# A scan and two feed-forward layers on one core: layer 0's second matrix laid side by side, and a new order of issue

## The chip, the core and the metric

The kernel runs on one core of a Trainium2 chip. The core has five engines that run side by side and wait for each other by semaphores: TensorE (PE) for matrix products, which it accumulates in PSUM; VectorE (DVE), ScalarE (ACT) and GpSimd (POOL) for element-wise work; and SyncE (SP), whose queue issues most of the DMAs between memory and SBUF. A matrix product is a pair of a weight load (PEld) and a matmul. The metric is the device time of one execution in microseconds, the median of three runs.

## What is computed

Inputs are four sequences of 768 tokens with 8 heads of width 32. First a scan with a decaying state, in chunks; then two feed-forward layers of width 256 with a hidden width of 1024, each with a residual; the first has a layer norm ahead, the second a mixing of tokens by a product of two thin matrices.

```python
for c in range(nc):                              # chunks of the scan, per batch and head
    cum = np.cumsum(la, axis=-1)
    L = np.exp(cum[:, :, :, None] - cum[:, :, None, :]) * causal
    y_intra = ((Cc @ Bc.T) * L) @ xc
    y_inter = (Cc @ state) * np.exp(cum)[:, :, :, None]
    state = decay_full * state + sum_j(Bc_j * xc_j * decay_from_j)
    y[:, :, sl] = y_intra + y_inter
# layer 0                                        # layer 1
xn = (x - mu) / np.sqrt(var + 1e-06) * g_ln      u = x + (x.T @ U @ V).T
x = x + np.maximum(xn @ w_ch1, 0.0) @ w_ch2      out = u + np.maximum(u @ w_ch1, 0.0) @ w_ch2
```

## The kernel before, in words

**Attention.** The tokens are cut into 24 chunks of 128 (6 for each sequence). For each chunk PE makes C times B (`cb`), DVE scans the decays (`lt`, L833) and multiplies (`mm`), PE makes the chunk's output (`yps`) and the new state (`sps`, then `gst` on DVE), and ACT and DVE split the output into a high and a low part (`yhl`), since every product of a layer is made of float32r numbers in two parts. PE also transposes the output (`tps`) for the residual and the norm.

**Layers.** A layer works on blocks of 256 or 512 tokens, in the order that `ORDER` gives for both layers together. For each of the 8 blocks f of 128 hidden units it makes `hps` (`mm1`, L1099: six products, in which the high and low parts of weights and tokens are combined), ACT makes the high part of its positive values (`hh`, L1106), DVE the low part (`hl`, L1110), and `mm2` adds the second product to `acc`. In layer 0 `mm2` runs for each 128 tokens. For the keys in `WIDE` one product of 512 columns (L1124) takes the high and the low part of the second matrix at once, and one of 256 columns (L1126) adds `hl` times the high part; the two halves of `acc` are added at the end on DVE (`y1`, `y2`, L1177). The other keys take three products of 256 columns (L1131). Layer 1 uses L1137. There are 128 products of L1124: 16 tiles of 128 tokens in the wide keys, times 8 blocks.

**The second matrix of layer 0** is one tile `w02` in SBUF, [128, 2, NF, DM]: part, block f, column. Its four pieces (`w2_piece`) are loaded as 64-bit words (`raw`), converted by ACT (L493, L497) and DVE (L502), and split: ACT writes the high part (`hi`, L393), DVE the low part (`lo`, L396). L1124 reads `weights["w2"][:, :, f, :]`: two runs of 256 elements, 8 KB apart.

**Between the layers** comes `mixing`: a thin product (`gps`), its copy (`gp`), a product that spreads it (`rps`), its high and low parts (`gsk`), then `ups` (transposes L1231 and products L1234), which ACT and DVE turn into the high and low parts of layer 1's input (`uhl`) and a copy (`u`).

**What sets the order.** The kernel does not write its instructions in the order of the program. Each piece of work is added to a `Plan` with its engine, a cost, what it waits for, the PSUM banks that it takes from a ring of eight (`m`) and a due time. `issue` then runs through time with these costs and places on each engine the ready piece that is due first. Due times come from `ffn` for products (from `T0` on) and backwards along the dependencies for the rest; then `SHIFT` moves whole kinds of pieces, `OFFSET` single ones, and `FIRST` puts some loads at the head in its own order. `NEAR` is how far ahead of the earliest start a piece may be and still be preferred, `STAY` a bonus for staying with the kind of product that PE is at. Two loads of `FIRST` (`cst0` and `ra` of the first chunks, by `ACTQ`) go by ACT's queue, the others by SP's.

Of the kernel before, what the change touches and what calls it, by code (L numbers as in the profile page):

```python
# [9 lines left out]
F32R = mybir.dt.float32r  # L10
# [11 lines left out]
NF = DFF // 128  # L22
# [8 lines left out]
FIRST = ['cst0', ('bc0', 0), 'rows', ('ra', 0, 0), ('stk', 0), ('xb', 0), (('w1', 0, 1), 'ld'), ('stk', 2),  # L31
         'cst', (('w1', 0, 0), 'ld'), (('w2', 0, 0), 'ld'), ('ra', 0, 2)]
# [10 lines left out]
OFFSET = {(('w1', 1, 1), 'ld'): 62.3, ('scan', 7, 0): 59.5, ('cb', 10, 0): 17.4, (('w1', 1, 2), 'ld'): 45.7,  # L43
# [6 lines left out]
          ('mm2', 0, (3, 0), 7): 48.4, ('tps', 18): -13.2, ('mean', 0): 3.2, ('state', 16): 3.2, ('cb', 15, 1): 8.1,  # L50
          ('mm2', 0, (1, 0), 2): 46.4, ('ylo', 17): 43.7, ('ras', 2, 3): 38.2, ('mm2', 1, (1, 1), 6): 18.4,
          ('mm2', 1, (1, 0), 6): 6.2, ('mm1', 1, (1, 0), 7): -7.5, ('ulo', (3, 0), 0): -5.0,
          ('mm2', 0, (0, 1), 0): -45.1, ('rep', 0): 22.0, ('cb', 13, 0): 13.0, ('mult', 3, 0): -35.8, ('tps', 8): 17.2,
          ('yhi', 8): -8.5, ('ulo', (1, 1), 1): 2.6, ('intra', 11): -18.9, ('acc', 1, (0, 1), 0): 20.3,
          ('state', 6): -7.8, ('ras', 2, 1): 1.3, ('bw', 1): -5.5, ('mm1', 0, (0, 1), 3): 19.1,
          ('hh', 0, (3, 0), 1): 0.3, ('gps', (3, 0)): -21.7, ('mm1', 1, (1, 1), 6): 7.7, ('bw', 10): 35.8,
          ('mult', 5, 0): -7.8, ('yhi', 14): 10.2, ('state', 8): -28.0, ('yc', 1): -27.8, ('mm1', 0, (1, 0), 7): -5.0,
          ('stk', 17): 23.2, ('ras', 2, 5): -5.1, ('mm1', 1, (0, 1), 5): 14.4, ('intra', 6): -34.5,
          ('mm2', 1, (1, 0), 3): 26.3, ('mm2', 0, (0, 1), 7): -33.3, 'dummy': 2.9, ('scan', 0, 0): 12.3,
          ('gsk', 0): 57.9, ('hl', 0, (0, 0), 3): -24.5, ('cb', 16, 0): 3.1, ('cb', 17, 0): -17.1,  # L60
          ('mm2', 1, (2, 1), 0): 11.1, ('ras', 2, 2): -6.6, ('state', 1): -28.0, ('state', 13): 15.9, ('gst', 1): -3.6,
          ('yhi', 7): -29.8, ('bc', 23): -34.6, (('w2', 0, 1), 's'): 10.4, ('mean', 8): -8.0,
          ('mm1', 0, (0, 0), 1): -28.9, ('state', 3): -86.4, ('tps', 23): -12.3, ('scan', 13, 1): -3.4,
          ('cd_', 2, 0): -11.7, ('yhi', 10): -33.1, (('w2', 1, 3), 'a'): -20.4, ('state', 19): -60.8,
          ('mm1', 0, (0, 0), 0): -34.7, (('w2', 1, 0), 's'): -45.9, (('w2', 1, 2), 's'): -35.8,
          ('mm1', 1, (3, 0), 3): -35.1, ('ylo', 5): -1.2, ('mult', 17, 1): -4.6, ('mult', 11, 0): -25.2,
# [11 lines left out]
          ('stk', 13): -2.8, ('sqrt', (0, 1)): 13.6, ('newton', (1, 1)): 38.2, ('y2', (0, 0), 1): 10.7,  # L78
# [7 lines left out]
          ('out', (3, 1), 1, 0): 13.5, ('acc', 1, (3, 0), 0): -27.5, ('out', (1, 0), 1, 0): -22.2,  # L86
          ('p2', (3, 1), 1, 0): 0.8, ('yhi', 5): -11.5, ('ylo', 18): -5.2, ('scan', 21, 0): 33.9,
# [4 lines left out]
          ('mm2', 0, (0, 0), 6): -1.6, ('sqrt', (3, 1)): -2.4, ('state', 22): -55.2, ('uhi', (0, 1), 1): 9.9,  # L92
          ('rst', 0, 0): -0.1, ('mult', 10, 0): -7.1, ('scan', 12, 0): 8.0, ('mm2', 1, (0, 1), 2): 0.2,
          ('tps', 20): -8.7, (('w1', 1, 3), 'f'): 18.9, (('v', 0), 'l'): 17.9, ('hh', 1, (1, 0), 6): 0.3,
          ('var', 23): -2.9, ('bcz', 0): -16.0, ('mm1', 1, (2, 1), 5): 29.3, ('mm1', 0, (3, 0), 5): 5.4,
          ('uhi', (2, 0), 1): 8.0, ('ras', 3, 0): 4.4, ('gst', 4): -2.3, ('slo', 2, 0): -4.0,
# [51 lines left out]
         "000 001 010 011 101 110 021 111 030 031 121 130 131".split()]  # L148


LAT, PER, T0, NEAR, SWITCH, STAY = 0.287, 1, -15.1, 0.11, 0.056, 2.68
dve = lambda n: 0.065 + n / 960
scn = lambda n: 0.06 + n / 480
dve2 = lambda n: 0.065 + n / 1920
# [1226 lines left out]
```

## Time and profile before

| | |
|---|---|
| median of 3 runs | 362.39 us (361.13, 362.39, 363.9) |
| the profiled execution's own time | 362.53 us |
| its span, first to last instruction | 360.3 us |
| PE busy | 352.9 us, 98% |
| DVE, ACT, POOL busy | 236.9, 160.8, 41.3 us |

A row of the trace is a group of instructions with its start, its busy time, engine, line and tile. Matmuls are pipelined and their ends are modelled, so the next one starts before the record of one ends: what a product costs in a stream is the step from start to start. "Idle before" is time in which the engine had nothing, with the engine and tile that ended it.

### The profile page before, as it was taken

To read this page: it belongs to the slowest core of one execution; us is meant where nothing else is said; L and a number is where in the kernel's file an instruction comes from. 1 tells how busy PE (TensorE), PEld (TensorE's weight loads), DVE (VectorE), ACT (ScalarE), POOL (GpSimd) and SP (SyncE) were. 2 spreads that over 40 slices of the span, in tenths; PEclk is the share of its full clock that TensorE was granted. 3 is DMA by queue.
4 is the path that set the end of the run, shared out by engine and by line. 5 is a ranking of instruction groups with operands and counts; after the bars stand their busy time and mean duration, and the time that the engine had idled before them with its cause. 6 is when DMAs were issued, how large, how long until landed. Compare 5 with 4: busy or idle time off the path is not lost.

```text
span 360.3 us, 7505 instructions
## 1 busy us (share of the span) xinstructions
PE 352.9 (98%) x2939; PEld 282.6 (78%) x2939; DVE 236.9 (66%) x503; ACT 160.8 (45%) x425; POOL 41.3 (11%) x44
## 2 busy tenths in 40 slices
PE   8999999999999999999999999999999999999995
PEld 4677787777799968877788888777787878888884
DVE  6888999989995545857998363867553562432423
ACT  3799665768853412425362121424423443231311
POOL 5545825202000000000030000000000000000000
PEclk9999999999999999999999999999999999999999
DMA  6999536474554436036452201715000000100101
GB/s 175 301 263 247 164 120 205 125 243 131 201 220 133 178 129 204 24 126 183 129 157 69 65 0 41 208 58 169 3 0 1 3 0 0 60 0 0 38 22 58
DMA packets 29592, 40.10 MB, mean 111 GB/s; under 512 B 3838, under 2 KB 19758, under 8 KB 29558
## 3 DMA queue, kind: packets, MB, share of 16 engines
q1 hardware_dynamic: 28982, 39.20, 34.9%
q8 instruction: 23, 0.38, 0.4%
q10 hardware_dynamic: 576, 0.43, 0.4%
q14 instruction: 11, 0.09, 0.1%
HBM read 31.67 MB, written 7.95 MB: 110 GB/s over the span
## 4 chain that ended last, share of the span: by engine, by line
PE 79%; DVE 9%; DMA 5%; ACT 3%; issue 2%; SPq 1%; DVEq 0%; ACTq 0%
PE hps L1099 32%; PE acc L1137 18%; PE acc L1124 7%; PE acc L1126 4%; PE acc L1131 3%; DMA raw<-in_w 3%; DMA lt<-arows 2%; PE yps L903 2%; PE cb L849 2%; DVE lt L833 2%; PE pc L523 2%; PE ups L1231 2%; DVE w L502 2%; PE tps L1025 1%; DVE hl L1110 1%
## 5 line engine op out<-in xcount | busy, mean ns | idle before, releaser
L1110 DVE SCALAR_TENSOR_TENSOR hl<-hps,hh 128x512 fp32r<-128x512 f32 (+1 forms) x104 | 66.4, 643 | 71.4 <-ACT hh L1106 71.2
L1106 ACT ACTIVATE hh<-hps 128x512 fp32r<-128x512 f32 (+1 forms) x104 | 58.3, 565 | 117.9 <-PE hps L1099 89.3
L1099 PE MATMUL hps<-yhl,w 128*128 128x512 f32 (+1 forms) x336 | 71.2, 364 | 0.6 <-DVE hl L1110 0.6
L1099 PE MATMUL hps<-uhl,w 128*128 128x512 f32 x288 | 69.3, 392 | 0.0
L1099 PEld LDWEIGHTS hps<-yhl,w 128*128 128x128 f32 x336 | 55.7, 189 | 11.8 <-DVE hl L1110 1.1
L1137 PE MATMUL acc<-hh,w 128*128 128x512 f32 x192 | 63.1, 392 | 0.0
L1099 PEld LDWEIGHTS hps<-uhl,w 128*128 128x128 f32 x288 | 53.4, 188 | 11.2 <-issue 0.2
L1124 PE MATMUL acc<-w,hh 128*128 128x512 f32 x128 | 47.6, 408 | 0.4 <-DVE hl L1110 0.3
L1137 PEld LDWEIGHTS acc<-hh,w 128*128 128x128 f32 x192 | 36.1, 188 | 7.4
L833 DVE TENSOR_TENSOR_SCAN lt<-lt,eye 128x512 f32<-128x512 f32 x32 | 39.3, 1239 | 3.5 <-DMA lt<-arows 3.4
L1137 PE MATMUL acc<-hl,w 128*128 128x512 f32 x96 | 37.4, 390 | 0.0
L1126 PE MATMUL acc<-w,hl 128*128 128x256 f32 x128 | 36.0, 281 | 0.2 <-DVE hl L1110 0.2
L807 POOL TENSOR_SCALAR stp<-stp,parity 128x256 f32<-128x256 f32 x23 | 28.2, 1240 | 22.5 <-DMA stp<-in_cbT 22.5
L1124 PEld LDWEIGHTS acc<-w,hh 128*128 128x128 f32 x128 | 24.0, 188 | 6.6 <-DVE hl L1110 0.5
L1126 PEld LDWEIGHTS acc<-w,hl 128*128 128x128 f32 x128 | 24.2, 189 | 0.9 <-DVE hl L1110 0.6
L1131 PE MATMUL acc<-w,hh 128*128 128x256 f32 x128 | 23.4, 283 | 0.0
L862 DVE TENSOR_TENSOR mm<-cb,lt 128x512 f32<-128x512 f32 x24 | 15.9, 687 | 7.7 <-PE cb L849 7.3
L1137 PEld LDWEIGHTS acc<-hl,w 128*128 128x128 f32 x96 | 18.1, 188 | 3.6
L1131 PEld LDWEIGHTS acc<-w,hh 128*128 128x128 f32 x128 | 20.3, 191 | 0.5
L602 POOL TENSOR_SCALAR ra<-ra 128x768 f32<-128x768 f32 x3 | 8.3, 2778 | 100.4 <-DMA ra<-in_a_rep 100.4
L1131 PE MATMUL acc<-w,hl 128*128 128x256 f32 x64 | 18.2, 285 | 0.0
L1177 DVE SCALAR_TENSOR_TENSOR yt<-acc,vrq,yt 128x256 f32<-128x256 f32 x40 | 17.2, 475 | 0.8 <-PE acc L1126 0.6
(110 smaller groups left out, 412.3 us busy)
## 6 DMA issues: line engine op xcount, KB each, us to landing
raw<-in_w SPq DMA_DIRECT2D x16, 512.0 KB, 5.2
lt<-arows SPq DMA_DIRECT2D x12, 512.0 KB, 4.9
stk<-st SPq DMA_DIRECT2D x48, 96.0 KB, 2.5
st<-sh SPq DMA_DIRECT2D x8, 384.0 KB, 3.0
xt<-in_xb SPq DMA_DIRECT2D x14, 192.0 KB, 3.7
lt<-arows SPq DMA_DIRECT2D x16, 128.0 KB, 4.8
xt<-in_xb SPq DMA_DIRECT2D x20, 96.0 KB, 3.7
stp<-in_cbT SPq DMA_DIRECT2D x12, 128.0 KB, 2.9
```

The lines of the kernel that those rows point to most:

```text
L602: eng.tensor_scalar(out=t, in0=t, scalar1=1e-6, scalar2=1.0, op0=ALU.max, op1=ALU.min)
L807: eng.tensor_scalar(out=t[:, 2 + i], in0=t[:, 1], scalar1=m, scalar2=None, op0=ALU.mult)
L833: V.tensor_tensor_scan(t, pair[k] if k < ROWS else t, eye, 0.0, op0=ALU.mult, op1=ALU.add)
L862: V.tensor_tensor(out=mm_[k][:, s_], in0=cbp[k, hf], in1=lt[k][:, s_], op=ALU.mult)
L1099: P.matmul(p[:, :n], w[:, k, fs], x[:, k, :], start=(i == 0), stop=(i == 5))
L1106: A.activation(out=hh[:, :n], in_=hps[l, key, f][:, :n], func=AF.Relu)
L1110: V.scalar_tensor_tensor(out=hl[:, :n], in0=hps[l, key, f][:, :n], scalar=0.0, in1=f32(hh[:, :n]), op0=ALU.max, op1=ALU.subtract)
L1124: P.matmul(accs[l, key][t], hh[:, at], weights["w2"][:, :, f, :], start=f == 0, stop=f == NF - 1, skip_group_check=True)
L1126: P.matmul(accs[l, key][t][:, DM:], hl[:, at], wh[:, f, :], start=False, stop=f == NF - 1, skip_group_check=True)
L1131: P.matmul(p, x[:, t * C:(t + 1) * C], w[:, f, :], start=(f == 0 and i == 0 and t % 2 == 0), stop=(f == NF - 1 and i == 2), skip_group_che ...
L1137: P.matmul(accs[l, key][d][:, :n], w[:, f, ds_], x[:, :n], start=(f == 0 and i == 0), stop=(f == NF - 1 and i == 2))
L1177: V.scalar_tensor_tensor(out=y, in0=p, scalar=rs[key]["r"][:, t:t + 1], in1=y, op0=ALU.mult, op1=ALU.add)
```

## The change

The tile of the second matrix becomes [128, NF, 2, DM]: for each block f the high and the low part lie side by side, and the wide product reads 512 elements in one run. The pieces are written with a step accordingly. The tables that set the order are replaced: `FIRST`, `OFFSET`, `T0`, `NEAR`, `STAY`, `SHIFT`. No operation is added or taken away. All lines of the changed kernel below `OFFSET` stand 4 later (L1128 for L1124).

```diff
-FIRST = ['cst0', ('bc0', 0), 'rows', ('ra', 0, 0), ('stk', 0), ('xb', 0), (('w1', 0, 1), 'ld'), ('stk', 2),
-         'cst', (('w1', 0, 0), 'ld'), (('w2', 0, 0), 'ld'), ('ra', 0, 2)]
+FIRST = [('bc0', 0), 'rows', ('stk', 0), ('xb', 0), (('w1', 0, 1), 'ld'), 'cst', 'cst0', ('stk', 2),
+         (('w1', 0, 0), 'ld'), (('w2', 0, 0), 'ld'), ('ra', 0, 0), ('ra', 0, 2)]
...
-OFFSET = {(('w1', 1, 1), 'ld'): 62.3, ('scan', 7, 0): 59.5, ('cb', 10, 0): 17.4, (('w1', 1, 2), 'ld'): 45.7,
+OFFSET = {(('w1', 1, 1), 'ld'): 69.1, ('scan', 7, 0): 41.9, ('cb', 10, 0): 1.6, ('mm1', 0, (1, 0), 3): 35.6,
...
-LAT, PER, T0, NEAR, SWITCH, STAY = 0.287, 1, -15.1, 0.11, 0.056, 2.68
+LAT, PER, T0, NEAR, SWITCH, STAY = 0.287, 1, 30.06, 0.108, 0.056, 1.03
...
-SHIFT = dict(zip("rows w0 w1 w2 ra0 ra chunk0 chunk".split(), [66.15, -409.01, -205.47, -39.12, -215.37, 82.47, -69.63, -11.6]))
+SHIFT = dict(zip("rows w0 w1 w2 ra0 ra chunk0 chunk".split(), [75.25, -477.95, -201.44, -29.96, -245.32, 76.45, -91.11, -12.35]))
...
-                weights["w2"] = const.tile([128, 2, NF, DM], F32R, tag="w02", name="w02")
-            return weights["w2"][:, i - 2]
+                weights["w2"] = const.tile([128, NF, 2, DM], F32R, tag="w02", name="w02")
+            return weights["w2"][:, :, i - 2]
...
-                        P.matmul(accs[l, key][t], hh[:, at], weights["w2"][:, :, f, :], start=f == 0, stop=f == NF - 1,
+                        P.matmul(accs[l, key][t], hh[:, at], weights["w2"][:, f].rearrange("p h d -> p (h d)"), start=f == 0, stop=f == NF - 1,
```

What the tables do to the order is seen on three places. Of the other engines' orders, SP's first rows differ in one pair (the load `cst` stands ahead of the second load of `stp` instead of behind it), and after that some loads of weight pieces, of `xt` and of `lt` change places by one or two.

**DVE, in the last blocks of layer 0's third group of tokens (`hl` with 256 columns).** `w<-w,raw` (L502) is the merge of a weight piece, `w<-w,w` the low part of one, `lt` the scan of a chunk. Before:

```order
L396 TENSOR_TENSOR yhl<-yps,yhl 128x2x64 x2
L396 TENSOR_TENSOR w_1071<-w_1482,w_991 128x512
L502 SCALAR_TENSOR_TENSOR w_1683<-w_1683,raw_1587 128x512
L1110 SCALAR_TENSOR_TENSOR hl<-hps,hh 128x256 x2
L833 SCALAR_TENSOR_TENSOR lt<-lt,eye 128x512
```

Now:

```order
L1114 SCALAR_TENSOR_TENSOR hl<-hps,hh 128x256
L506 SCALAR_TENSOR_TENSOR w_1589<-w_1589,raw_1349 128x512
L1114 SCALAR_TENSOR_TENSOR hl<-hps,hh 128x256
L400 TENSOR_TENSOR yhl<-yps,yhl 128x2x64 x2
L400 TENSOR_TENSOR w_1071<-w_1398,w_1021 128x2x256
L400 TENSOR_TENSOR w_1173<-w_1589,w_1153 128x512
L1114 SCALAR_TENSOR_TENSOR hl<-hps,hh 128x256
```

Before, two `hl` stood behind a merge; now one `hl` stands ahead of a merge, one behind it and one behind two more operations.

**PE, in the same blocks.** `acc<-w_369,hh` is the wide product, `hps` the first product of a block. Before:

```order
L924 MATMUL yps<-mm,xt_93 32x64 x16
L1124 MATMUL acc<-w_369,hh 128x512
L1126 MATMUL acc<-w_369,hl 128x256
L1124 MATMUL acc<-w_369,hh 128x512
L1126 MATMUL acc<-w_369,hl 128x256
L1099 MATMUL hps<-yhl,w_384 128x256
L1099 MATMUL hps<-yhl,w_301 128x256 x2
```

Now:

```order
L928 MATMUL yps<-mm,xt_93 32x64 x16
L1103 MATMUL hps<-yhl,w_384 128x256
L1103 MATMUL hps<-yhl,w_301 128x256 x2
L1103 MATMUL hps<-yhl,w_384 128x256
L1103 MATMUL hps<-yhl,w_301 128x256 x2
L1128 MATMUL acc<-w_369,hh 128x512
L1130 MATMUL acc<-w_369,hl 128x256
```

The pairs of the wide product moved behind a block of `hps`.

**PE, where the first mixing product `ups` for layer 1 stands.** Before, it stands among the `acc` products of the next block of tokens:

```order
L1131 MATMUL acc<-w_369,hh 128x256 x2
L1131 MATMUL acc<-w_369,hl 128x256
L1231 MATMUL ups<-cst,yt 128x128 x8
L1234 MATMUL ups<-vs,gsk 128x512 x2
L1131 MATMUL acc<-w_369,hh 128x256 x2
```

Now, among its `hps` products, after the second of five blocks:

```order
L1103 MATMUL hps<-yhl,w_384 128x512
L1103 MATMUL hps<-yhl,w_301 128x512 x2
L1235 MATMUL ups<-cst,yt 128x128 x8
L1238 MATMUL ups<-vs,gsk 128x512 x2
L1103 MATMUL hps<-yhl,w_384 128x512
```

It moved ahead of three blocks of `hps` and two of `acc`.

## Rows read from the trace of the kernel before

**Rows 1.** The page: busy time of the engines; the granted clock by slices.
```profile
PE 352.9 (98%) x2939; PEld 282.6 (78%) x2939; DVE 236.9 (66%) x503; ACT 160.8 (45%) x425; POOL 41.3 (11%) x44
PEclk9999999999999999999999999999999999999999
```

**Rows 2.** Stretches: length, then busy us and instructions of each engine, clock, DMA.
```profile
0.00:36.00 36.00, 34.14 (x496) 23.89 (x497) 29.16 (x74) 27.29 (x72) 19.36 (x29) 1.00 0.89 246
36.00:90.00 54.00, 52.47 (x843) 41.84 (x843) 52.19 (x127) 37.00 (x105) 19.17 (x15) 1.00 0.53 165
90.00:108.00 18.00, 17.75 (x166) 15.34 (x165) 17.02 (x32) 12.52 (x33) 0.00 (x0) 1.00 0.56 212
108.00:342.00 234.00, 234.00 (x1378) 189.86 (x1377) 133.63 (x265) 81.40 (x213) 2.77 (x1) 1.00 0.24 76
342.00:360.30 18.30, 14.56 (x65) 11.72 (x63) 4.89 (x9) 2.63 (x5) 0.00 (x0) 1.00 0.13 43
```

**Rows 3.** PE's waits: for whom, us in total, times, longest.
```profile
PE hps L1099 <- DVE hl L1110: 0.6, 1, 0.6
...
PE acc L1124 <- DVE w L396: 0.2, 1, 0.2
```

**Rows 4.** Groups by line and shape: count, busy us, mean ns, idle before.
```profile
L1137 PE MATMUL acc<-hh,w 128*128 128x512 f32 x192 | 63.1, 392 | 0.0
L1124 PE MATMUL acc<-w,hh 128*128 128x512 f32 x128 | 47.6, 408 | 0.4 <-DVE hl L1110 0.3 <-DVE w L396 0.2
L396 DVE TENSOR_TENSOR w<-w,w 128x512 fp32r<-128x512 f32 x12 | 8.1, 678 | 0.1
L393 ACT ACTIVATE w<-w 128x512 fp32r<-128x512 f32 x12 | 7.6, 633 | 4.9 <-DVE w L502 4.9
```

**Rows 5.** Timeline of PE: start, busy us; first of sixteen pairs, and what follows.
```profile
187.72 0.39 PE L1124 MATMUL acc<-w,hh 128*128 128x512 f32 x1
...
193.36 0.86 PE L1099 MATMUL hps<-yhl,w 128*128 128x512 f32 x3
```

**Rows 6.** The chain that ended last: start, us, what.
```profile
37.07 1.02 PE cb L844 x16
...
96.74 6.83 PE hps L1099 x30
103.57 2.88 PE acc L1131 x24
...
216.16 5.44 PE acc L1137 x24
```

**Rows 7.** Timeline of the start: the load of constants, POOL's parts, PE's reader.
```profile
5.53 0.43 SPq L378 DMA_DIRECT2D cst<-in_consts  x1
...
10.73 3.84 POOL L807 TENSOR_SCALAR stp<-stp,parity 128x256 f32<-128x256 f32 x4 [2.80 <-DMA stp<-in_cbT]
...
19.57 1.09 PE L844 MATMUL cb<-stp 64*64 64x256 f32 x16
```

**Rows 8.** Timeline of PE near 92 us.
```profile
91.92 0.39 PE L1124 MATMUL acc<-w,hh 128*128 128x512 f32 x1
92.56 0.39 PE L1126 MATMUL acc<-w,hl 128*128 128x256 f32 x1 [0.25 <-DVE hl L1110]
```

**Rows 9.** Timeline of DVE near 92 us.
```profile
91.48 0.69 DVE L502 SCALAR_TENSOR_TENSOR w<-w,raw 128x512 int32<-128x512 int32 x1 [0.85 <-ACT raw L497]
92.09 0.75 DVE L1110 SCALAR_TENSOR_TENSOR hl<-hps,hh 128x256 fp32r<-128x256 f32 x2
```

**Rows 10.** Timeline of all engines from 96 to 112 us.
```profile
96.31 1.65 DVE L1177 SCALAR_TENSOR_TENSOR yt<-acc,vrq,yt 128x256 f32<-128x256 f32 x4
...
99.06 0.68 DVE L1110 SCALAR_TENSOR_TENSOR hl<-hps,hh 128x512 fp32r<-128x512 f32 x1
...
107.07 0.71 PE L1234 MATMUL ups<-vs,gsk 128*128 128x512 f32 x2
...
110.52 1.13 ACT L393 ACTIVATE u<-ups 128x512 f32<-128x512 f32 x2 [1.85 <-DVE uhl L396]
```

More of the change, by code (lines that the diff above doesn't have):

```diff
@@ L42 @@
 FIRST_TWO = [('w1', 0, 0), ('w1', 0, 1)]
-OFFSET = {(('w1', 1, 1), 'ld'): 62.3, ('scan', 7, 0): 59.5, ('cb', 10, 0): 17.4, (('w1', 1, 2), 'ld'): 45.7,
[6 rows of a table removed]
[L50 to L66, printed above, removed]
[11 rows of a table removed]
-          ('stk', 13): -2.8, ('sqrt', (0, 1)): 13.6, ('newton', (1, 1)): 38.2, ('y2', (0, 0), 1): 10.7,
[7 rows of a table removed]
-          ('out', (3, 1), 1, 0): 13.5, ('acc', 1, (3, 0), 0): -27.5, ('out', (1, 0), 1, 0): -22.2,
-          ('p2', (3, 1), 1, 0): 0.8, ('yhi', 5): -11.5, ('ylo', 18): -5.2, ('scan', 21, 0): 33.9,
[4 rows of a table removed]
[L92 to L96, printed above, removed]
[15 rows of a table removed]
-          ('ylo', 6): 2.4, ('bc', 17): 19.0, ('gps', (2, 1)): -13.3, ('yhi', 23): 15.5, ('ulo', (1, 0), 1): -9.8,
[7 rows of a table removed]
-          ('ylo', 4): 1.9, 'starts': -20.3, ('tps', 15): 7.4, ('yc', 6): 16.8, 'clip': -14.9, ('uhi', (0, 0), 1): 13.5,
[6 rows of a table removed]
-          ('mm2', 0, (0, 0), 5): 1.6, ('yhi', 2): 10.6, ('scan', 9, 0): -5.3, ('yhi', 3): -1.6, ('mult', 2, 0): 2.4,
[9 rows of a table removed]
-          ('gp', (0, 0)): -3.0, ('mult', 18, 0): 1.7, ('ras', 0, 0): -2.2, ('tps', 13): 1.5, ('stw', 3, 0, 2): 0.2,
-          ('yhi', 15): 4.6, ('scan', 14, 0): -1.8, (('w1', 1, 1), 'l'): -0.3, ('mm1', 0, (3, 1), 7): 0.2,
-          ('hh', 1, (1, 0), 5): 0.1, ('uhi', (3, 0), 1): -4.5, ('cd_', 3, 0): 0.9, ('scan', 17, 1): -0.5,
[5 rows of a table removed]
@@ new lines @@
+OFFSET = {(('w1', 1, 1), 'ld'): 69.1, ('scan', 7, 0): 41.9, ('cb', 10, 0): 1.6, ('mm1', 0, (1, 0), 3): 35.6,
+          ('mm2', 0, (0, 1), 4): 90.1, ('cb', 4, 0): 10.4, (('w2', 1, 0), 'l'): -22.0, ('state', 15): 8.4,
+          ('mm1', 1, (0, 1), 4): 77.3, ('state', 11): 17.1, ('intra', 12): -4.4, ('gps', (1, 0)): 27.8,
[5 rows of a table added]
+          'zero': 3.0, ('cb', 13, 0): 15.0, ('tps', 8): 17.2, ('ulo', (1, 1), 1): 4.6, ('intra', 11): -4.7,
+          ('acc', 1, (0, 1), 0): 20.3, ('state', 6): -8.3, ('mm1', 0, (0, 1), 3): 18.9, ('mm1', 1, (1, 1), 6): 7.7,
+          ('mult', 5, 0): -12.3, ('state', 8): -36.4, ('tps', 14): -8.2, ('yc', 1): -31.5, ('mm1', 0, (1, 0), 7): -1.6,
[4 rows of a table added]
+          ('mm1', 0, (0, 0), 1): -35.9, ('state', 3): -78.8, ('scan', 13, 1): -3.4, ('yhi', 10): -38.2,
[5 rows of a table added]
+          ('hl', 1, (0, 1), 1): -27.7, ('scan', 11, 0): 2.7, ('ras', 2, 4): -23.8, ('scan', 22, 1): 7.2,
+          ('var', 10): 15.6, ('mm1', 1, (3, 0), 1): -7.8, ('yc', 13): 16.5, ('mm2', 0, (1, 0), 3): -3.1,
+          ('mm1', 1, (1, 1), 5): -35.6, ('hl', 0, (0, 1), 7): 2.7, ('cb', 23, 0): -17.0, ('mm1', 1, (0, 1), 2): 12.3,
+          ('hh', 0, (0, 1), 5): -5.1, ('yhi', 21): 18.5, ('stk', 13): 3.3, ('acc', 1, (3, 1), 1): 0.0,
[9 rows of a table added]
+          ('hl', 0, (1, 1), 3): 36.0, ('acc', 0, (1, 0), 1): 26.9, ('state', 20): -12.7, ('acc', 1, (1, 0), 0): -11.1,
[5 rows of a table added]
+          ('ylo', 13): 12.9, ('cb', 22, 1): 4.3, ('acc', 1, (2, 1), 0): 1.3, ('ylo', 6): 12.9, ('gps', (2, 1)): -14.1,
[3 rows of a table added]
+          ('acc', 1, (1, 0), 1): -19.5, ('tps', 21): -10.0, 'starts': -12.0, ('tps', 15): 7.4, ('yc', 6): 16.8,
[5 rows of a table added]
+          ('ylo', 22): -15.8, ('shi', 2, 1): 23.1, ('hh', 1, (3, 0), 3): 4.5, ('mean', 11): -5.9, ('ylo', 15): -3.6,
[13 rows of a table added]
+          ('intra', 15): 1.0, ('hh', 1, (1, 0), 6): 24.0, ('ylo', 20): 13.4, ('gm', 0): 0.3, ('mean', 17): -3.7,
[7 rows of a table added]
+          ('mm2', 1, (1, 1), 1): -4.9, ('ylo', 14): 0.9, ('stw', 3, 0, 2): 8.7, ('acc', 0, (0, 1), 1): 1.5,
[3 rows of a table added]
+          ('rep', 2): -10.6, ('out', (2, 1), 1, 0): 11.8, ('hh', 0, (2, 1), 0): 0.2, ('stm', 20): 18.3,
+          ('mm1', 1, (3, 0), 2): -4.4, ('gp', (3, 0)): -2.8, ('stk', 15): -3.8, ('mean', 15): -2.8,
+          ('gps', (3, 1)): 0.4, ('acc', 0, (3, 0), 1): 0.3, ('tps', 20): -1.0, ('part', 4, 3): -11.6,
+          ('ras', 3, 1): -10.1, ('mean', 23): -1.5, ('stw', 2, 0, 2): 12.3, (('w2', 0, 0), 'a'): 4.4,
+          ('bc', 22): -12.0, ('hh', 1, (1, 1), 6): -16.7, ('hh', 1, (0, 1), 2): -2.9, ('scan', 21, 0): 11.6,
+          ('ups', (0, 0), 0): -8.7, ('mean', 5): -7.7, ('hh', 0, (1, 1), 3): 0.9, ('stw', 3, 0, 1): 6.3,
+          ('yc', 7): -8.6, (('w2', 1, 3), 'h'): -6.1, ('sqrt', (2, 1)): -5.7, ('mult', 18, 1): 1.8, ('gst', 12): -1.6,
+          ('stk', 22): 7.3, ('var', 5): -3.9, ('intra', 19): -2.4, ('var', 9): -6.5, ('ulo', (2, 0), 0): -12.6,
+          ('y1', (3, 1), 3): 3.2, ('hl', 0, (1, 0), 5): -14.1, ('mm1', 0, (3, 0), 4): -8.1, (('w1', 0, 2), 'p'): -5.4,
+          ('acc', 1, (1, 1), 1): -16.3, ('stw', 3, 1, 2): -6.4, ('p2', (0, 0), 1, 0): -4.5, ('mult', 21, 1): -6.2,
[5 rows of a table added]
+          ('scan', 3, 0): -4.2, ('intra', 3): 1.0, ('intra', 5): 8.5, ('mm1', 0, (1, 1), 7): 2.3, ('cd', 0): 9.8,
[14 rows of a table added]
```

148 rows, old and new, of the table OFFSET are left out of this document.

## The prediction

> **What bounds the kernel now.** I read the page's busy shares first, then the table of stretches, then the list of what PE waited for, then single products. [...] The stretches say where the rest lies: from 108 to 342 us PE is busy 234.00 of 234.00, so nothing there can be late for it; the not-busy time is 1.86 us before 36, 1.53 us between 36 and 90, 0.25 us between 90 and 108, and 3.74 us in the last stretch, which is the drain after the last product [rows 2]. VectorE (DVE) is the second: 52.19 of 54 us between 36 and 90 and 17.02 of 18 between 90 and 108, but 134 of 234 after that [rows 2]. So the end is set by the sum of PE's products, plus what DVE makes PE wait for before 108. The waits view names eight waits of PE beside the start, from 0.6 down to 0.2 us [rows 3]. A matmul's record is longer than the step to the next one (0.39 against 0.227 us below), so each wait can hide up to 0.16 us more: 8 x 0.16 = 1.3 us. All that a better order can win on PE after 36 us is therefore about 1.53 + 0.25 + 1.3 = 3.1 us.
>
> **The count of instructions.** Both programs issue the same number of instructions of each line on each engine, the fillers at the start included, and groups of layer products and of attention products alternate 90 times on PE before and 92 times now. No term comes from removed or added work.
>
> **The layout.** 128 wide products (L1124) take 512 columns that lie in two runs of 256 elements, 8 KB apart; now they lie in one run. A record of theirs means 408 ns, a 512-column product whose columns lie together (L1137) 392 ns [rows 4]. Durations overlap, so I take the step instead. Sixteen pairs L1124 and L1126 stand back to back from 187.72 to 193.36 us [rows 5]: 5.64/16 = 352.5 ns a pair. Contiguous products cost 5.44/24 = 226.7 ns for 512 columns and 2.88/24 = 120.0 ns for 256 [rows 6], so a contiguous pair should cost 346.7 ns. The difference, 5.8 ns, times 128 is 0.74 us, all on the engine that sets the end. Bounds: zero, if the pair is slow for another reason than its strip, and 128 x 16 ns = 2.0 us by the records. I take 0.8, by the step, since the step is what adds up.
> [...]
> The other side of the edit: the pieces of layer 0's second matrix are now written as two runs instead of one. That is 4 conversions on ScalarE (ACT) and 4 subtractions on DVE. The rows of these lines already mix one-run and two-run writes, and mean 633 and 678 ns [rows 4]. I see no cost; were it 50 ns each, 4 x 0.05 = 0.2 us would fall on DVE while it is nearly full. Zero.
>
> **The start.** PE's own order is word for word the same up to the third group of cb products at 37.07 us [rows 6]; only then does a sps group change its place. On SP's queue one load of constants is moved ahead of a pair of stp loads. Its issue takes 0.43 us, so stp lands that much later; POOL, which waits 2.80 us for it, would start at 11.2 instead of 10.7 and end at 15.0, and PE reads the result at 19.57 us [rows 7]. Covered by 4.5 us; without that cover it would cost the 0.43. On DVE two pairs of small operations swap, with the same end. Zero for this stretch, so its 1.86 us stay.
>
> **The moved products before 96 us.** Here is the one wait that the new order goes at. From 91.92 to 92.56 PE takes 0.64 us for a product whose step is else about 0.23 (the pair less 0.12), waiting for an hl [rows 8]. That hl stands on DVE behind a merge of a weight piece (L502), and DVE stood idle 0.85 us until ACT had made its input [rows 9]. In the new order an hl stands ahead of such a merge and another behind it, the last of these loads stands one place earlier on SP, and PE places twelve more 256-column products ahead of four pairs. I count this wait as gone: 0.64 - 0.23 = 0.4 us. Bounds: 0 to 3.1 us won, as above; lost, if a merge is late in its new place too, the same 0.85 us of idle DVE in front of one hl. I stay near the small end, because only this one place shows both the cause and its removal. If it goes, the next late thing is the scan L833 behind it on DVE, which no product needs at once.
>
> **The move of ups.** PE issued the mixing products ups behind 30 hps and 24 acc products; now they stand between the second and third block of hps. They are the same products, 0 on PE itself. But ups takes two of the eight PSUM banks until ACT has copied u out: from 107.78 to 111.65 us, 3.9 us [rows 10]. Four y additions (96.31, 1.65 us), which free two banks of the previous sum, are spread on DVE behind two hl, a subtraction over 768 columns and each other. Two of the sum, two of ups and five of hps would be nine. Cover: five hps blocks take 6.83 us on PE [rows 6], so with ups (some 1.3 us) ahead of it the fifth is wanted at about 96.7 + 4 x 1.37 + 1.3 = 103.5 us, and before, DVE's first hl of the five began at 99.06 [rows 10]; even a few microseconds behind that a bank is free. I take 0; if the cover is gone PE waits at most the 3.9 us for which ups holds its banks. Queued behind it would be all of PE.
>
> **After 108 us** PE never stands, and DVE is busy 57% of the time [rows 2]. The order there changes who goes first and not the sum. Two more changes between kinds of products cost some 0.1 us each. Zero.
>
> **Sum.** -0.8 (layout) -0.4 (one wait) + 0 = -1.2 us. The profiled execution took 362.53 us, 2.2 us around its span of 360.3, and is 0.1 us above the median 362.39. So 362.4 - 1.2 = 361.2 us.
>
> **The rivals.**
> *The strip is free.* The pair's 5.8 ns come from mixing a 512- with a 256-column product and not from the break; then only 0.4 us are left, 362.0 us. For it: there is no wide contiguous pair in this trace. Against it: the 16 ns between two 512-column lines that both change weights each time. [...] Chance 0.25.
> *The order takes all of PE's waits.* 0.8 + 3.1 = 3.9 us, 358.5 us. For it: weight pieces, the cause of the 0.85 us, are loaded and merged earlier in several places. Against it: DVE is busy 97% where the waits lie, and a queue that full has little room for everything to be early. Chance 0.13.
> *Banks run out behind ups (slower).* PE stands at the fifth hps block until u is copied. It decides from 0.8 us of standing on, where it eats the layout's gain; the full 3.9 us give 362.4 - 0.8 + 3.9 = 365.5 us, and with a free strip 366.3. For it: nine banks wanted of eight, and y additions moved back on a full DVE. Against it: the 4 us between the first hl and the fifth block. Chance 0.15.
> *The forecast*, 361.2 us: 0.47.
>
> **How the numbers follow.** A measurement of this kernel can tell about 1% from no change; the three runs before spread over 2.8 us. One per cent is 3.6 us, that is under 358.8 or over 366.0. Faster by more needs the whole second rival and a little luck or its layout at more than the step: 0.12. Slower by more needs the full wait for banks and a free strip, or two such places: 0.10. Within 1%: 0.78. The likeliest case's own range is 360.2 to 362.4. The range for 8 in 10 runs from 358.9, just above the second rival, to 365.2, most of the way to the third.
>
> **What would show it.** The layout is right if L1124's records mean about 392 ns and sixteen pairs take 5.55 us; it is wrong if they stay at 408 or rise. The order is right if PE's not-busy time between 36 and 108 falls from 1.78 us by some 0.3, and the wait at an acc product for hl near 92 us is gone. The third rival shows as an hps product with an idle time of over 1 us before it, released by an hl, a y addition or a copy of u, near 100 to 107 us. The prediction would be wrong if a stretch after 108 us showed PE standing at all, or if a raw load landed so late that several hl follow it.

## The result: 0.7% slower, and nothing from the layout

| | before | after |
|---|---|---|
| median | 361.76 us (22 runs) | 363.60 us (22 runs) |
| ratio, 95% interval | | 1.0066 (1.0045 to 1.0087) |
| profiled execution, its span | 362.53, 360.3 us | 364.4, 362.1 us |

The forecast was 361.2 us, 0.3% under the kernel before. By its median the changed kernel is 1.8 us slower than the kernel before and 2.4 us over the forecast, still within 1%. The medians alone differ by 0.5%; the ratio stands higher because some executions of the changed kernel are much slower than its others (the means are 364.02 and 361.64 us). Its stretches, with the columns of [rows 2]:

```profile
0.00:36.00 36.00, 33.42 (x495) 23.45 (x496) 29.31 (x74) 27.33 (x72) 19.22 (x29) 1.00 0.90 247
36.00:90.00 54.00, 50.27 (x813) 40.08 (x819) 49.08 (x121) 35.95 (x102) 19.84 (x15) 1.00 0.52 158
90.00:108.00 18.00, 18.00 (x195) 15.65 (x195) 17.82 (x35) 13.65 (x34) 0.00 (x0) 1.00 0.64 231
108.00:342.00 234.00, 234.00 (x1382) 189.50 (x1382) 135.37 (x267) 79.62 (x214) 2.83 (x1) 1.00 0.25 76
342.00:362.10 20.10, 16.45 (x73) 13.30 (x71) 5.59 (x10) 3.59 (x6) 0.00 (x0) 1.00 0.10 33
```

Only one stretch stands out against [rows 2]: between 36 and 90 us PE is now not busy for 3.73 us, where it was 1.53. That is 2.2 us, more than the whole difference of the spans (1.8 us). From 90 us on PE never stands until the drain. And DVE, which was busy 52.19 of those 54 us, is busy 49.08: it stands too, three microseconds longer. What PE and DVE wait for (us in total, times, longest; three of PE's, then the transfer for which DVE waits most):

```profile
PE acc L1135 <- DVE hl L1114: 1.4, 1, 1.4
...
PE hps L1103 <- DVE hl L1114: 0.9, 1, 0.9
PE hps L1103 <- DVE yhl L400: 0.7, 1, 0.7
```
```profile
DVE bw L884 <- DMA xt<-in_xb: 4.2, 3, 2.9
```

In the kernel before, PE's longest wait beside the start was 0.6 us [rows 3], and no wait of DVE for xt is in its list. The place of the 1.4 us, on SP, DVE and PE of the changed kernel (start, busy us):

```profile
66.45 0.38 SPq L382 DMA_DIRECT2D raw<-in_w  x1
67.39 1.11 SPq L382 DMA_DIRECT2D xt<-in_xb  x2
...
69.93 1.05 DVE L647 TENSOR_TENSOR_SCAN ra<-ra,zero 128x128 f32<-128x128 f32 x3
73.84 0.29 DVE L884 TENSOR_TENSOR bw<-xt,lt 128x128 f32<-128x128 f32 x1 [2.86 <-DMA xt<-in_xb]
74.05 0.68 DVE L506 SCALAR_TENSOR_TENSOR w<-w,raw 128x512 int32<-128x512 int32 x1
74.65 0.68 DVE L1114 SCALAR_TENSOR_TENSOR hl<-hps,hh 128x512 fp32r<-128x512 f32 x1
...
75.39 0.39 PE L1135 MATMUL acc<-w,hl 128*128 128x256 f32 x1 [1.38 <-DVE hl L1114]
```

And the transfer itself, from the chain of waits of the same kernel (start, us, what):

```profile
67.95 5.86 DMA xt<-in_xb
```

Read the first of the two from the bottom. PE wants the hl of the last block of pair (0,1). That hl stands on DVE behind a merge of a weight piece (L506) and behind bw, which multiplies chunk 10's xt. DVE stood 2.86 us at bw until xt landed, 5.86 us after its second part was sent. And xt went out on SP just behind a raw load, 512 KB of a layer-1 weight. Here is the same place in the kernel before:

```profile
67.26 1.11 SPq L378 DMA_DIRECT2D xt<-in_xb  x2
69.10 0.75 SPq L378 DMA_DIRECT2D raw<-in_w  x1
...
72.60 0.69 DVE L1110 SCALAR_TENSOR_TENSOR hl<-hps,hh 128x512 fp32r<-128x512 f32 x1
73.20 0.28 DVE L880 TENSOR_TENSOR bw<-xt,lt 128x128 f32<-128x128 f32 x1
```

There the raw load goes out behind xt, hl stands ahead of bw, and bw waits for nothing. So two moves of the new order meet at this place: one on SP, one on DVE.

A second place of the same kind, with 0.7 us of PE, follows near 86 us: chunk 11's bw waits 0.86 us for its xt (SP sent it at 80.75 us, behind two raw loads whose issue took 5.89 us), and behind it stand vs and yhl; PE waits for that yhl.

### The profile page after: what moved, and what is told of

Its sections match the earlier page's. It is cut to its first block, busy times and chain, and to the rows that moved or that the text cites. A ratio compares the mean times of both kernels' runs of the same rounds, so it can differ in the third digit from the quotient of the medians.

```text
span 362.1 us, 7522 instructions
## 1 busy us (share of the span) xinstructions
PE 352.1 (97%) x2939; PEld 282.0 (78%) x2939; DVE 237.2 (65%) x503; ACT 160.1 (44%) x425; POOL 41.9 (12%) x44
## 4 chain that ended last, share of the span: by engine, by line
PE 77%; DVE 9%; DMA 9%; issue 2%; SPq 1%; ACT 1%; DVEq 0%; POOL 0%; ACTq 0%; POOLq 0%
PE hps L1103 32%; PE acc L1141 18%; PE acc L1128 7%; PE acc L1130 3%; DMA raw<-in_w 3%; PE acc L1135 3%; DMA xt<-in_xb 3%; PE cb L853 2%; PE yps L907 2%; PE ups L1235 2%; DVE hl L1114 2%; DVE lt L837 1%; DVE w L506 1%; DMA stp<-in_cbT 1%; SPq L382 1%
## 5 line engine op out<-in xcount | busy, mean ns | idle before, releaser
L1128 PE MATMUL acc<-w,hh 128*128 128x512 f32 x128 | 47.9, 410 | 0.4 <-DVE hl L1114 0.4
L1128 PEld LDWEIGHTS acc<-w,hh 128*128 128x128 f32 x128 | 24.1, 188 | 7.0 <-issue 1.2
L606 POOL TENSOR_SCALAR ra<-ra 128x768 f32<-128x768 f32 x3 | 8.7, 2895 | 101.6 <-DVE vrq L1062 99.8
```

The source lines that it names most:

```text
L606: eng.tensor_scalar(out=t, in0=t, scalar1=1e-6, scalar2=1.0, op0=ALU.max, op1=ALU.min)
L1128: P.matmul(accs[l, key][t], hh[:, at], weights["w2"][:, f].rearrange("p h d -> p (h d)"), start=f == 0, stop=f == NF - 1, skip_group_check ...
```

## The experiments

Theory O: the loss is the new order's, and the layout is free. Theory Q, its mechanism: instructions of PE's chain stand on DVE behind one that waits for a transfer, and that transfer is late behind a raw load. Rivals: the layout costs; PE stands for another reason; the loss is spread over the order.

Most kernels here take the finished list of instructions and move one or a few of them; nothing else changes. In the short diffs `move A behind B` stands for such a move: `('xb', 10)` is the load of chunk 10's xt, `(('w1', 1, 3), 'ld')` the raw load of a piece of layer 1's first matrix, `('bc', 11)` and `('bc', 12)` the loads of lt, `('hl', 0, (0, 1), 7)` the hl above. All ratios are to the kernel before, run again beside each group of kernels, with the 95% interval, from 12 runs of the kernel named (xt_later: 6).

### Layout alone, order alone

layout_only is the kernel before with the layout:

```diff
-weights["w2"] = const.tile([128, 2, NF, DM], ...)
+weights["w2"] = const.tile([128, NF, 2, DM], ...)
...
```

> The kernel before with the three lines of the new layout and none of the new order. Theory O (the loss is the order's, the side-by-side strip is free): ratio 1.000 within 0.002, the wide product's records at 408 to 410 ns, its pair still 351 to 353 ns, PE's standing between 36 and 90 us still about 1.5 us. Rival L (the layout costs: weights written in two runs, or read from a strip that suits TensorE worse): ratio 1.003 to 1.007. By the step of the forecast (the wide product gets 0.8 us cheaper in all): ratio 0.998 and records at 392 ns.

Measured: 0.9989 (0.9971 to 1.0008). order_only is the changed kernel with those lines put back:

```diff
-weights["w2"] = const.tile([128, NF, 2, DM], ...)
+weights["w2"] = const.tile([128, 2, NF, DM], ...)
...
```

> The changed kernel with the old layout put back: only the new order is left. Theory O: ratio 1.005 to 1.009, as the whole change has (1.0066), and the same waits of DVE for xt near 74 and 86 us (2.9 and 0.9 us). Rival L: ratio 1.000 to 1.003, since what costs is taken out.

Measured: 1.0047 (1.0024 to 1.0071). The loss goes with the order. The intervals of the first leave room for a small gain by the layout, but the traces do not. The wide products after 108 us, where PE never stands (records in ns, shortest/median/longest; first and last start in us), of the kernel before, of layout_only, of the changed kernel and of order_only:

```profile
L1124 PE MATMUL acc<-w,hh x96: 387/396/578, 187.7 to 286.7; 128*128 128x512 f32 x96
```
```profile
L1124 PE MATMUL acc<-w,hh x96: 387/396/577, 184.6 to 283.8; 128*128 128x512 f32 x96
```
```profile
L1128 PE MATMUL acc<-w,hh x96: 389/398/577, 189.7 to 289.6; 128*128 128x512 f32 x96
```
```profile
L1128 PE MATMUL acc<-w,hh x96: 389/398/577, 186.5 to 286.3; 128*128 128x512 f32 x96
```

In the order before, 96 of the 128 wide products and all that stands between them take 99.0 us with the broken strip and 99.2 with the whole one; in the new order 99.9 with the whole and 99.8 with the broken one. The median record is the same within each pair, too. The mean that the prediction went by, 408 ns before [rows 4], does not fall either (layout_only, then the changed kernel):

```profile
L1124 PE MATMUL acc<-w,hh 128*128 128x512 f32 x128 | 47.5, 407 | 0.0
```
```profile
L1128 PE MATMUL acc<-w,hh 128*128 128x512 f32 x128 | 47.9, 410 | 0.4 <-DVE hl L1114 0.4
```

The layout is worth nothing that these figures can tell.

The profiled execution of order_only, the fastest of its 12, did not show the long wait: DVE stood 1.16 us for xt where 2.9 were expected, and PE had its hl. Nor did layout_only's, the fastest of its 12 too, show the 1.5 us of standing that its order, the one before, had in [rows 2]. The stretch of layout_only, then of order_only:

```profile
36.00:90.00 54.00, 53.75 (x859) 43.81 (x857) 52.73 (x131) 39.94 (x111) 19.86 (x14) 1.00 0.56 176
```
```profile
36.00:90.00 54.00, 52.87 (x853) 42.92 (x853) 51.98 (x129) 38.65 (x110) 20.30 (x15) 1.00 0.55 174
```

PE stands 0.25 and 1.13 us here, where the same two orders stood 1.53 and 3.73. So how late xt lands and how long PE stands differ from one execution to the next; from here on verdicts rest on the ratios, and a trace shows only by what way a loss can come.

### The two moves put into the kernel before

bw_front moves bw, load_late the raw load, load_late_bw both:

```diff
+move ('bw', 10) ahead ('hl', 0, (0, 1), 7)         # bw_front, load_late_bw
+move (('w1', 1, 3), 'ld') ahead ('xb', 10)         # load_late, load_late_bw
```

> The kernel before with the two suspected moves alone: the raw load ahead of chunk 10's xt on SP, and chunk 10's bw ahead of the hl on DVE; layout and all the rest as before. Theory Q: DVE waits 0.5 to 1.5 us for xt near 73 us and PE for the hl behind it 0.3 to 1.3 us, ratio 1.001 to 1.004. Rival N (the loss is spread over the order): ratio 1.000 within 0.001.

> The kernel before with one DVE instruction moved, as the new order has it: chunk 10's bw ahead of the hl, and the raw load where it was, behind xt. Both moves together gave 1.0058. Theory Q2 (it takes both: a wait for xt only costs with a late xt, and a late xt only costs with bw ahead of hl): bw finds its xt landed or waits under 0.5 us, ratio 1.000 to 1.002. Rival B (bw ahead of hl is enough by itself, since xt lands late in many executions anyway): ratio 1.004 to 1.006.

> The kernel before with one transfer moved, as the new order has it: the raw load ahead of chunk 10's xt on SP, with bw behind hl as before. Theory Q2: DVE waits up to 1 us for xt behind the hl, PE has its hl and doesn't stand near 74 us, ratio 1.000 to 1.002. Rival R (the transfer ahead is enough by itself): ratio 1.004 to 1.006.

| ratio | raw load behind xt | raw load ahead of xt |
|---|---|---|
| hl ahead of bw | 1 (before) | 1.0007 (0.9983 to 1.0032) |
| bw ahead of hl | 1.0005 (0.9974 to 1.0036) | 1.0058 (1.0036 to 1.0079) |

Each move alone costs nothing that can be measured; both together cost nearly what the whole change costs, and more than the 1.001 to 1.004 expected. (The interval of bw_front ends at 1.0036, where that of both begins; load_late's ends below it.) DVE at this place in load_late_bw with the product that waits, then in load_late, then in bw_front:

```profile
73.48 0.29 DVE L890 TENSOR_TENSOR bw<-xt,lt 128x128 f32<-128x128 f32 x1 [1.29 <-DMA xt<-in_xb]
73.69 0.68 DVE L1120 SCALAR_TENSOR_TENSOR hl<-hps,hh 128x512 fp32r<-128x512 f32 x1
...
74.43 0.39 PE L1141 MATMUL acc<-w,hl 128*128 128x256 f32 x1 [1.06 <-DVE hl L1120]
```
```profile
70.65 0.69 DVE L1119 SCALAR_TENSOR_TENSOR hl<-hps,hh 128x512 fp32r<-128x512 f32 x1
71.98 0.29 DVE L889 TENSOR_TENSOR bw<-xt,lt 128x128 f32<-128x128 f32 x1 [0.64 <-DMA xt<-in_xb]
```
```profile
71.83 0.29 DVE L889 TENSOR_TENSOR bw<-xt,lt 128x128 f32<-128x128 f32 x1
72.04 0.68 DVE L1119 SCALAR_TENSOR_TENSOR hl<-hps,hh 128x512 fp32r<-128x512 f32 x1
```

With both, DVE waits at bw and PE at the hl behind it. With the late load alone DVE waits too, 0.64 us, but behind hl, and PE has what it needs. With bw in front alone xt has landed. In load_late_bw's trace 1.06 us is the wait shown; another hl cost PE 0.55 us near 95 us, behind a DVE wait of 1.52 us for lt, so how the full 2 us come together is not shown by one trace.

How late the raw load makes xt can be read from all traces. Where it stands behind xt, chunk 10's xt takes 2.7 to 3.4 us from issue to landing (the kernel before, layout_only, bw_front, load_early and raw_last); where it stands ahead, 3.3 to 6.2 us (the changed kernel, order_only, bw_behind, load_late and load_late_bw). SP can add to that: in load_late_bw xt was sent some 2 us later than in the kernel before, because the issue of two raw loads ahead of it took 5.10 us.

```profile
64.00 5.10 SPq L388 DMA_DIRECT2D raw<-in_w  x2
69.20 1.52 SPq L388 DMA_DIRECT2D xt<-in_xb  x2
```

### The places mended in the changed kernel

bw_behind takes back DVE's move, load_early SP's:

```diff
+move ('bw', 10) behind ('hl', 0, (0, 1), 7)        # bw_behind
+move (('w1', 1, 3), 'ld') behind ('xb', 10)        # load_early
```

> The changed kernel with one DVE instruction moved: chunk 10's bw stands behind the hl that it stood ahead of, the raw load stays ahead of xt. Theory Q: PE's wait of 1.38 us for that hl near 75 us is gone; DVE still waits for xt, 1 to 2 us, and what it waits out then comes in front of the next hl instead, which has some 2 us of room, so the time falls by 0.7 to 1.3 us: ratio 1.003 to 1.005. Rival P (PE's standing there is due to something else that is late by as much): wait and ratio unchanged, 1.0066.

Measured: 1.0013 (0.9996 to 1.0030). One DVE instruction behind another instead of ahead of it gives back most of the loss, more than the 1.003 to 1.005 expected of theory Q. PE's wait for hl near 75 us is not in its trace; nor is a wait of DVE for this xt, of which 1 to 2 us were expected.

> The changed kernel with one transfer moved on SP: the load of a layer-1 weight part (raw, 128x2x512) that now goes out just ahead of chunk 10's xt goes out just behind it, as it did before the change. Theory Q (the xt is late because a raw load is ahead of it, and bw, which waits for it, holds back the hl behind it on DVE): DVE's wait for xt near 74 us falls from 2.86 to under 1.5 us, PE's wait for hl there from 1.38 to under 0.3 us, the time by 1.0 to 1.4 us to a ratio of 1.003 to 1.004. Rival N (the xt is late whatever is ahead of it, by the freeing of its buffer or by the load of all transfers): wait and ratio unchanged, 1.0066.

Measured: 1.0050 (1.0028 to 1.0071), in theory Q's direction but short of the 1.003 to 1.004 expected, and its interval still holds the 1.0066 of the changed kernel. The trace shows a way: DVE no longer waits at bw, but 4 us later.

```profile
74.52 1.22 DVE L846 TENSOR_TENSOR_SCAN lt<-lt,eye 128x512 f32<-128x512 f32 x1 [1.75 <-DMA lt<-arows]
...
77.89 0.44 PE L1038 MATMUL tps<-cst,yc 128*128 128x128 f32 x2 [0.71 <-DVE yt L1190]
```

The raw load now stood ahead of the lt transfers, as in the kernel before, where DVE waits 0.96 us for lt; the scan waits for them, and a y addition that PE needs stands behind the scan. In these two traces DVE's long wait is for the transfer that stands next behind the raw load on the queue: 2.86 us for xt in the changed kernel, 1.75 us for lt here. By what way the raw load makes it late is not shown. raw_last moves the load behind lt too:

```diff
+move (('w1', 1, 3), 'ld') behind ('bc', 12)
```

> The changed kernel with the one raw load moved on SP behind xt and behind the three lt transfers after it; bw stays ahead of hl on DVE. With the raw load between xt and lt (load_early) the ratio was 1.0050, and DVE waited 1.75 us for lt instead of 2.86 us for xt. Theory H (the raw load makes late whatever stands behind it, and what DVE does next waits for that): with nothing of chunk 10 and 11 behind it DVE waits under 0.5 us for xt and for lt near 74 us, PE's wait for hl near 75 us is gone, and the ratio is 1.000 to 1.003. Rival S (the raw load hardly matters in the changed kernel; xt and lt are late through other transfers): DVE still waits over 1 us for one of them, ratio 1.004 to 1.007.

Measured: 1.0018 (0.9998 to 1.0038), with bw still ahead of hl. DVE's wait at this place:

```profile
70.39 0.29 DVE L893 TENSOR_TENSOR bw<-xt,lt 128x128 f32<-128x128 f32 x1 [0.27 <-DMA xt<-in_xb]
```

So from SP's side as from DVE's side most of the loss can be taken away, and by about the same amount; both intervals lie wholly below that of the changed kernel. PE still stands 2.10 us between 36 and 90 us in raw_last's trace, at other places.

What is left, 0.1 to 0.2%, I tried to take away with two more kernels:

```diff
+move ('bw', 10) behind ('hl', 0, (0, 1), 7)        # bw_vs, mended
+move (('v', 1), 'l') ahead ('bw', 11)
+move ('v', (1, 0)) ahead ('bw', 11)
+move (('w1', 1, 3), 'ld') behind ('bc', 12)        # mended alone
```

> The kernel with bw behind hl, and a second place mended: vs (second half) and yhl of pair (1,0) now stand ahead of chunk 11's bw, which waits for the next xt, as they did before the change in effect. Theory Q (what the order lost is instructions of PE's chain standing on DVE behind a bw that waits for a transfer): PE's wait of 0.55 to 0.65 us for yhl near 86 us is gone, and the time falls by 0.5 to 0.7 us against bw_behind, to a ratio of 0.999 to 1.000. Rival N (the loss is spread over many places of the order): the wait goes but returns at the next hl, ratio still 1.001 to 1.003.

> The changed kernel with all the suspected places mended: bw behind hl, vs and yhl ahead of chunk 11's bw, and the raw load behind xt and behind the lt transfers too, so that neither is late (with the raw load between xt and lt, DVE waited 1.75 us for lt). Theory Q: no wait of DVE for xt or lt over 0.5 us near 74 and 85 us, PE stands under 1 us between 36 and 108 us, ratio 0.998 to 1.001. Rival N (what is left of the new order costs by itself): ratio 1.002 to 1.005.

Measured: 1.0020 (0.9992 to 1.0048) and 1.0018 (0.9994 to 1.0043), where 0.999 to 1.000 and 0.998 to 1.001 were expected. The moves are not quite what the expectation says: `('v', (1, 0))` is a small operation of the layer norm (vrq), and yhl stays behind bw in both. But vs, 1.1 us of DVE's time, now fills the time until xt lands, and DVE no longer waits at bw (bw_vs):

```profile
84.06 0.28 DVE L895 TENSOR_TENSOR bw<-xt,lt 128x128 f32<-128x128 f32 x1
84.26 0.48 DVE L411 TENSOR_TENSOR yhl<-yps,yhl 128x128 fp32r<-128x128 f32 x2
```

The wait of hps for yhl near 86 us is gone in both (in bw_vs a product of chunk 11 waits 0.36 us for yhl there instead), but the ratio stays: the second place was no part of the loss that can be told apart. In mended PE stands 2.18 us between 36 and 90 us, where under 1 us was expected: 0.68 us at hps near 63 us, 0.69 us for hl near 79 us, the latter now behind ACT, and 0.49 us near 82 us. The last two are in raw_last's trace too (0.89 and 0.49 us) and not in those of bw_behind and bw_vs, which leave the raw load where it was; so that move seems to bring waits of its own. Whether the 0.1 to 0.2% that bw_behind, raw_last, bw_vs and mended have in common is real stays open: each of the four intervals holds 1, but all four ratios lie above it. The wait at hps near 63 us, 0.40 to 0.94 us in every trace of the new order and at most 0.57 us in those of the old, is a candidate that no run tests in the new order.

### The wait made longer

```diff
+move ('xb', 10) behind ('bc', 12)
```

> The suspected wait made longer: in the changed kernel chunk 10's xt goes out on SP behind three more transfers of lt (1.7 us of issue). Theory Q: DVE's wait for xt near 74 us grows from 2.9 to 4.5 to 5.5 us, PE's wait for hl from 1.4 to 3 to 3.5 us, the time by 1.7 to 2.2 us over the changed kernel: ratio 1.011 to 1.013; and if a long standing of PE also lowers the granted clock, as 6 of the 22 runs of the changed kernel at 0.993 to 0.995 suggest, the trace shows a slice at the lower level behind it and the ratio comes to 1.015 or more. Rival P (PE stands for another reason): PE's wait and ratio unchanged.

Measured: 1.0193 (1.0157 to 1.0228), 368.03 us. DVE and PE at the place, then the granted clock in single microseconds (the figure behind the busy times, 1.00 is full speed):

```profile
75.35 0.29 DVE L893 TENSOR_TENSOR bw<-xt,lt 128x128 f32<-128x128 f32 x1 [5.37 <-DMA xt<-in_xb]
...
76.90 0.39 PE L1144 MATMUL acc<-w,hl 128*128 128x256 f32 x1 [3.77 <-DVE hl L1123]
```
```profile
76.00:77.00 1.00, 0.10 (x1) 0.10 (x1) 1.00 (x3) 0.72 (x2) 0.00 (x0) 1.00 0.00 0
77.00:78.00 1.00, 1.00 (x8) 1.00 (x8) 1.00 (x4) 0.18 (x1) 0.00 (x0) 0.81 0.64 174
78.00:79.00 1.00, 1.00 (x6) 1.00 (x6) 1.00 (x2) 0.89 (x2) 0.00 (x0) 0.50 0.86 334
79.00:80.00 1.00, 1.00 (x7) 1.00 (x6) 1.00 (x3) 0.84 (x2) 0.00 (x0) 0.50 0.04 16
80.00:81.00 1.00, 1.00 (x7) 1.00 (x6) 1.00 (x4) 0.84 (x2) 0.00 (x0) 0.50 0.00 0
81.00:82.00 1.00, 1.00 (x59) 0.78 (x66) 1.00 (x3) 0.78 (x3) 0.00 (x0) 0.98 0.00 0
```

DVE's wait grew as expected, PE's a little more (5.37 and 3.77 us), and the time by more than they did: behind PE's standing the granted clock fell to 0.50 for some 3.5 us. The mean clock of that execution was 0.995, which over 364.5 us is 1.8 us. In the traces PE's longer wait (2.4 us more) and the clock together are 4.2 us; by the ratios xt_later is 4.6 us slower than the changed kernel.

### A version that should beat both

tuned takes the order before, the new layout, and goes at the waits of [rows 3], [rows 8] and [rows 9], and with its last line at DVE's 0.96 us for lt; two_moves is the same without that line:

```diff
+move ('scan', 10, 0) behind ('hl', 0, (0, 1), 5)
+move (('w1', 1, 1), 'f') behind ('hl', 0, (1, 0), 6)
+move (('w1', 1, 3), 'ld') behind ('bc', 12)        # tuned alone
```

> A version that should beat both: the order before, the new layout, and three moves: one scan behind the hl near 62 us (PE waits 0.57 us there before), a merge behind two hl near 92 us (0.25 us), and the raw load behind the lt transfers on SP (DVE waits 0.96 us for lt near 76 us). Theory Q: 0.6 to 0.9 us less than layout_only (0.9989), ratio 0.996 to 0.998. Rival N: waits reappear at the next hl, ratio 0.998 to 1.000.

> The kernel called tuned without its third move: the new layout on the order before, one scan behind the hl near 62 us and one merge behind two hl near 92 us; the raw load stays between xt and lt. If the raw load's move was what cost tuned its gain (1.0021 where 0.997 was expected): ratio 0.996 to 0.999. If one of the other two moves costs, or tuned's figure is the spread of its runs: ratio 1.000 to 1.003.

Measured: tuned 1.0021 (0.9997 to 1.0045), where 0.996 to 0.998 was expected, and two_moves 0.9985 (0.9957 to 1.0014). In both traces PE hardly stands between 36 and 108 us (0.46 and 0.17 us; the kernel before 1.78). That doesn't show that the moves did it, since layout_only, with none of them, stands 0.25 us there. And tuned isn't faster, and two_moves cannot be told from the kernel before: its median is 360.9 us beside 361.8. The two intervals overlap, so that the raw load's move is what costs tuned isn't shown. Nothing here is surely faster than the kernel before. Two_moves and layout_only come nearest, and the most that they promise is 0.4%.

## Why the prediction was wrong

**What bounds the kernel: right.** PE is busy 234.00 of 234.00 us from 108 to 342 us in both kernels, and what changed lies before 108, where DVE makes PE wait. The bound of 3.1 us was drawn too wide: of the eight waits that it counts, three end before 36 us (near 12, 16 and 32 us), and five give 1.53 + 0.25 + 0.8 = 2.6 us. That changes only the second rival, which did not come.

**The layout, -0.8 us: wrong.** It is 0.0. The step that failed is the price of the broken strip: the prediction took for it the 5.8 ns between a measured pair and a pair put together from separate streams, and the 16 ns between two lines' means, 408 and 392 ns [rows 4], as the evidence for it. By its own sign it is wrong: the mean did not fall to 392 but is 407 ns in layout_only and 410 in the changed kernel. With the whole strip sixteen pairs take 5.65 us (layout_only, 184.57 to 190.22 us) instead of 5.64 [rows 5], so the 5.8 ns belong to the change between 512 and 256 columns or to something else that both layouts share; which of the two is not shown. The first rival named this and was given 0.25. The other side of the edit, the writes in two runs, is free as forecast: the means of the two rows named for it are 633 and 683 ns in layout_only beside 633 and 678.

**The start, 0: not refuted.** The stretch before 36 us differs by over 2 us of busy PE between executions of kernels with the same start (34.14 before, 32.00 in tuned), so a single trace says nothing on a few tenths of a microsecond.

**The wait near 92 us, -0.4 us: right by mechanism, not seen in the time.** It is gone; PE is busy 18.00 of 18.00 us between 90 and 108. One trace would not show that, since layout_only has the old order and 18.00 too; but in that stretch PE stands 0.25 to 0.82 us in three of five traces of the old order, and at most 0.07 us in all eight of the new one. Its removal is not seen in the time, and two_moves, which removes it and another, gains 0.5 us by its ratio, with no change inside its interval.

**The moved products and loads before 96 us: the step that decided.** I looked only for places where a moved piece removes a wait, counted one, and bounded a loss by the one wait the trace showed, 0.85 us for a merge. Two moves were never costed: a raw load that stands ahead of xt on SP, and bw that stands ahead of an hl on DVE. Neither shows a wait in the trace before, and each alone costs nothing; I took rows without a wait as free. That a raw load stands one place earlier was even counted as a help; another raw load one place earlier, ahead of xt, did the harm. None of the three rivals had this way. The last sentence of the prediction did name a raw load that lands so late that several hl follow it; it was the transfer behind the raw load that was late.

**ups and the banks: right.** No hps product stands near 100 to 107 us, so the slower rival did not come, though a slower result did.

**After 108 us: right.** PE never stands until the drain in the changed kernel, nor in any other trace but load_late_bw's (0.21 us). The 0.1 us for a change between kinds of products can be read from the trace before: the first wide product behind yps takes 0.34 us to the next product (42.88 to 43.22 us), the one after it 0.23 us (43.34 to 43.57).

**The sum.** -1.2 us was forecast. Layout 0.0 instead of -0.8, order about +2 instead of -0.4: the two moves alone make 1.0058 where the whole change makes 1.0066, and either of them undone in the changed kernel (by DVE, or by SP with lt) leaves 1.0013 to 1.0018. That 363.6 us lies inside the range of 358.9 to 365.2 us is luck: its upper end was drawn for the wait for banks, which did not come.

## What to carry to other kernels

On an engine that works through its instructions in order, as DVE does here (in the changed kernel its 2.86 us at bw held up the hl behind it, and PE stood 1.38 us for that hl), what waits for a transfer belongs behind what the bounding engine needs next: there a wait of 0.64 us cost nothing that can be measured (load_late, 1.0007), and one move of this kind took the changed kernel from 1.0066 to 1.0013. A move of a load and a move of its reader have to be costed together: each was free, and the pair took 2 us. And a mean record of one line against another's is no price; a stretch of the same products with and without the edit is.

## What the runs showed of the hardware

In xt_later, when PE had stood 3.77 us for one hl, the granted clock went from 1.00 to 0.50 of full speed about a microsecond after PE had begun again at 76.90 us (0.81 from 77 to 78 us, 0.50 from 78 to 81), and stayed there for some 3.5 us of full work; the wait of 1.38 us in the changed kernel's trace did no such thing (1.00 from 70 to 90 us). All six executions of xt_later had a mean clock of 0.986 to 0.995. So in the traced execution the wait cost half as much again as it lasted: 3.77 us of standing and, as estimated from the mean clock of 0.995, 1.8 us of clock.

Six of the changed kernel's 22 executions had a mean clock of 0.993 to 0.995 and took 365.1 to 366.9 us. The other sixteen have a mean of 363.33 us, 1.0047 times that of the kernel before; that is the ratio of order_only, too, none of whose 12 had a low clock. So about 0.5% of the loss stands without the clock, and the six add the other 0.2%. That they are executions in which xt landed later than in the one shown is likely, but argued: no trace of such an execution of the changed kernel was taken. None of bw_behind's and raw_last's 12 had it; but one of 12 did in each of load_early, load_late_bw, bw_vs, mended and two_moves, and so did one of the kernel before's, so this wait need not be the only thing that brings it.
